# Normalising a tile in four interleaved steps instead of three, in the second layer of a fused attention and two-layer kernel

## The chip, the cores and the metric

One core of a Trainium2 chip runs the whole program: threshold attention, a first layer and a second layer. The metric is the device time of one execution in microseconds, the median of several. TensorE multiplies matrices into PSUM banks; VectorE, ScalarE and GpSimd do the element-wise work; SyncE issues the DMAs. Each engine takes its instructions strictly in the order in which the program gives them.

## The reference

The attention output becomes an array of 2304 rows of 512, then two layers follow. The change touches the second:

```
x = attention(q, k, v, tau)                    # -> (2304, 512)
g = where(h >= 1, h, where(h <= -1, 0, (h + 1)**2 / 4)),  h = x @ w_in1    # 2048 wide
x = g @ w_out1                                 # (2304, 512)

h   = x @ w_in2                                # (2304, 1024)
e   = exp(h - max(h));  sm = e / (sum(e) + 1e-9)          # per row
s   = h * sm
ln  = (s - mean(s)) / sqrt(var(s) + 1e-6) * g_ln
out = ln @ w_out2                              # (2304, 512)
```

## The kernel before

The first layer ends with an array x in SBUF, feature by token. The second layer takes the 2304 tokens as 18 tiles of 128, in 9 pairs. Each value is split in two halves, a high and a low one, and each product is three matmuls (high by high, high by low, low by high) over each part of the contraction.

**The first matrix product** of a pair k (tiles 2k and 2k+1) is done by seven half-sized products, `product(k, 1)` to `product(k, 7)` (L979), after the scheme that needs seven block products instead of eight. Each is six matmuls of 128x512. The left factors are sums of blocks of x: `y_adds` (L934) makes them on VectorE, four adds of 128x256, and `y_split` (L943) makes the high half on ScalarE (L948) and the low half on GpSimd (L949). `product(k, 1)` leaves its bank to a ScalarE copy (L994), and products 6, 7 and 4 add to the same bank afterwards; 5 is copied by L998 and 3 adds to its bank; 6 is copied by L1000. Products 2, 3 and 7 end in an add with a maximum on VectorE (L975), 4 in a maximum (L1006).

**The normalisation** of a tile i is a generator, `moe2_ln` (L1008), and `ln_step(i)` (L1210) issues it to the next yield. Step 1: the negative maximum on VectorE (L1015) and two exponentials with sums on ScalarE (L1018). Step 2: the sum and its reciprocal (L1022, L1023), two products h * e / sum with sums on VectorE (L1026), the mean (L1030) and a square with its sum on ScalarE (L1031). Step 3: the variance (L1033), its power -0.5 on GpSimd (L1034), a correction of three short instructions on VectorE (L1035 to L1037), the multiply over 128x1024 (L1038), and, for all but the two first and the two last tiles, `moe2_shuffle` (L1048): a VectorE transpose within blocks (L1052) and four DMA writes to DRAM (L1058).

**The second matrix product.** `moe2_fetch(i)` (L1066) loads a shuffled tile back in one DMA; `moe2_land(i)` (L1083) makes its high half on ScalarE (L1087) and its low half on GpSimd in two instructions (L1090). For the two first and the two last tiles `moe2_tr(i)` (L1095) does this with TensorE transposes instead, two ScalarE casts (L1108) and two VectorE subtractions (L1109). `moe2_out(i)` (L1126) is 24 matmuls (L1132), eight by eight: high by both halves of the weights, then low. `moe2_store(i)` (L1138) copies the bank on ScalarE (L1142) and issues the output DMAs on SyncE (L1144).

**The order.** The program is scheduled by hand: the order of the calls at the end of the kernel (L1281 to L1381) is each engine's order. Waits between engines come from the data dependencies. Pairs 0 to 2 are written out call by call; a loop over k = 3 to 8 follows (L1327), with o = 2k - 4, in which the products of pair k, the normalisation of tiles o+2 and o+3, the first step of tile 2k and the outputs o and o+1 stand side by side. "Output o" is `moe2_out(o)`, and (k,n) is `product(k, n)`. A part written out by hand follows the loop for the last tiles. `jobs.finish()` issues what is left of the preparation of the weights of the last product: in this execution one GpSimd subtraction (L552).

Of the kernel before, what the change touches and what calls it, by code (L numbers as in the profile page):

```python
# [21 lines left out]
def kernel(  # L22
# [82 lines left out]
    def f32(ap):  # L105
        return ap.bitcast(F32)
# [522 lines left out]
    def parts(*keys):  # L629
        return [lambda key=key, n=n: part(key, n) for key in keys for n in range(KD)]  # L630
# [66 lines left out]
    jobs = Jobs(parts(("in1", 0), ("out1", 0)), JOB_EVERY, 2)  # L697
# [29 lines left out]
    for b in range(B - 1):  # L727
        o = (b + 1) * NPAIR * UNITS
        at(late_, o + 6, recips_load, b, att_p)
        at(late_, o + 9, recips, b)  # L730
    for b in range(B - 1):
        for p in range(NPAIR):
            o = (b + 1) * NPAIR * UNITS + NORM[0] + NORM[1] * p
# [54 lines left out]
    X_AT, o = {}, 0  # L788
# [145 lines left out]
    def y_adds(k):  # L934
        r0, r1, pairs = y_views(k)
        a11, a12, a21, a22 = (x[:, h : h + KH, r] for r in (r0, r1) for h in (0, KH))
        s1, s2, s3, s4 = (t[:, h : h + KH, :] for t in pairs for h in (0, KH))
        nc.vector.tensor_tensor(s1, a21, a22, op=ALU.add)
        nc.vector.tensor_tensor(s3, a11, a21, op=ALU.subtract)
        nc.vector.tensor_tensor(s2, s1, a11, op=ALU.subtract)  # L940
        nc.vector.tensor_tensor(s4, a12, s2, op=ALU.subtract)

    def y_split(k, m):  # L943
        r0, r1, pairs = y_views(k)
        v = ([x[:, :, r0]] + pairs + [x[:, KH:KD, r1]])[m]
        n = v.shape[1]
        hi, lo = (t.rearrange("p (k t) -> p k t", k=n) for t in y_home(k, m))
        nc.scalar.copy(hi, v)  # L948
        nc.gpsimd.tensor_tensor(lo, v, f32(hi), op=ALU.subtract)  # L949
        for h in range(0, n, KH):  # L950
            y_t[k, 2 * m + h // KH] = hi[:, h : h + KH, :], lo[:, h : h + KH, :]
# [27 lines left out]
    def product(k, n):  # L979
        b, a, o = PRODUCTS[n]  # L980
        hi, lo = y_t[k, a]
        w = op_tile(o)
        ps = acc(k, b)
        first = n in (1, 2, 5)
        for kk in range(KH):
            for m, (st, at_) in enumerate(((hi, kk), (hi, KH + kk), (lo, kk))):
                nc.tensor.matmul(  # L987
                    ps, lhsT=st[:, kk, :], rhs=w[:, at_, :],
                    start=first and kk == 0 and m == 0, stop=kk == KH - 1 and m == 2,
                    skip_group_check=not first,  # L990
                )
        i = 2 * k
        if n == 1:
            nc.scalar.copy(so_half(i, 0), ps)  # L994
        elif n == 2:
            add_max(i, 0, ps)
        elif n == 5:
            nc.scalar.copy(so_half(i + 1, 1), ps)  # L998
        elif n == 6:
            nc.scalar.copy(so_half(i, 1), ps)  # L1000
        elif n == 7:
            add_max(i + 1, 1, ps)
        elif n == 3:
            add_max(i, 1, ps)
        else:
            nc.vector.tensor_reduce(maximum(i + 1, 0), ps, axis=AXES.X, op=ALU.max)  # L1006

    def moe2_ln(i):  # L1008
        st = g_p.tile([P, 10], F32, tag="st", name="st", bufs=3)
        e = keep["e"][:, i % 2, :]  # L1010
        so = keep["so"][i // 2 % 2][:, i % 2, :]
        half = [slice(HF * g, HF * g + HF) for g in range(2)]
        h = [so[:, half[0]] if i % 2 == 0 else acc_t[i // 2, 0], so[:, half[1]]]
        nmax, sm, mu, va, rs, t1 = (st[:, n : n + 1] for n in range(6))
        nc.vector.tensor_scalar(nmax, maximum(i, 0), maximum(i, 1), -1.0, op0=ALU.max, op1=ALU.mult)  # L1015
        two = [st[:, n : n + 1] for n in range(8, 10)]
        for g in range(2):
            nc.scalar.activation(  # L1018
                out=e[:, half[g]], in_=h[g], func=ACTF.Exp, bias=nmax, scale=1.0, accum_out=two[g]
            )  # L1020
        yield
        nc.vector.tensor_scalar(sm, two[0], two[1], 1e-9, op0=ALU.add, op1=ALU.add)  # L1022
        nc.vector.reciprocal(sm, sm)  # L1023
        two = [st[:, n : n + 1] for n in range(6, 8)]
        for g in range(2):
            nc.vector.scalar_tensor_tensor(  # L1026
                out=so[:, half[g]], in0=h[g], scalar=sm, in1=e[:, half[g]], op0=ALU.mult, op1=ALU.mult,
                accum_out=two[g],
            )
        nc.vector.tensor_scalar(mu, two[0], two[1], -1.0 / FF2, op0=ALU.add, op1=ALU.mult)  # L1030
        nc.scalar.activation(out=e, in_=so, func=ACTF.Square, bias=mu, scale=1.0, accum_out=va)  # L1031
        yield
        nc.vector.tensor_scalar(va, va, 1.0 / FF2, 1e-6, op0=ALU.mult, op1=ALU.add)  # L1033
        nc.gpsimd.tensor_tensor(rs, va, mhalf, op=ALU.pow)  # L1034
        nc.vector.tensor_scalar(t1, rs, rs, va, op0=ALU.mult, op1=ALU.mult)  # L1035
        nc.vector.tensor_scalar(t1, t1, -0.5, 1.5, op0=ALU.mult, op1=ALU.add)
        nc.vector.tensor_tensor(rs, rs, t1, op=ALU.mult)  # L1037
        nc.vector.tensor_scalar(so, so, mu, rs, op0=ALU.add, op1=ALU.mult)  # L1038
        ln_t[i] = e, so
        if i not in ON_PE:  # L1040
            moe2_shuffle(i)
        yield
# [23 lines left out]
    def moe2_fetch(i):  # L1066
        land = land_t[i] = raw_p.tile([P, FF2], F32, tag="raw", name="land")
        nc.sync.dma_start(land, sq_t.pop(i))
# [26 lines left out]
    def moe2_tr(i):  # L1095
        _, so = ln_t.pop(i)
        if i > 1:
            t = wga_p.tile([P, 2, FF2], F32R, tag="wg", name="ln")
            hi, lo = t[:, 0, :], [t[:, 1, 0:T], t[:, 1, T:FF2]]
        else:  # L1100
            hi, lo = split_tiles(i)
        for g in range(2):
            o = slice(T * g, T * g + T)
            ps = y_bank(3 + g if i == 0 else 1 + g, "lt")
            for f in range(KD):
                r = slice(f * P, f * P + P)
                nc.tensor.transpose(ps[:, r], so[:, T * g + f * P : T * g + f * P + P], ident)  # L1107
            nc.scalar.copy(hi[:, o], ps)  # L1108
            nc.vector.tensor_tensor(lo[g], ps, f32(hi[:, o]), op=ALU.subtract)  # L1109
        lt_t[i] = halves(hi, lo)  # L1110
# [27 lines left out]
    def moe2_store(i):  # L1138
        if i not in o_ps:
            return  # L1140
        o = wt_p.tile([P, DM], F32, tag="w", name="o")
        nc.scalar.copy(o, o_ps.pop(i))  # L1142
        for r, rows in out_rows(i):
            nc.sync.dma_start(rows, o[r, :])  # L1144
# [55 lines left out]
    jobs = Jobs([], 0, 3)  # L1200
# [9 lines left out]
    def ln_step(i):  # L1210
        if 0 <= i < NTT:
            if i not in ln:
                ln[i] = moe2_ln(i)
            next(ln[i])
# [68 lines left out]
    product(1, 1)  # L1283
    product(1, 5)
    ln_step(1)
    y_adds(2)
    product(1, 2)
    ln_step(0)
    product(1, 6)
    for m in range(2):  # L1290
        y_split(2, m)
# [1 line left out]
    product(1, 3)  # L1293
    product(1, 7)
    moe2_tr(0)
    ln_step(1)
    for m in range(2, 4):
        y_split(2, m)
    jobs.finish()
    ln_step(2)  # L1300
    product(2, 1)
    ln_step(2)
    ln_step(2)
    moe2_fetch(2)
    product(2, 2)
    product(1, 4)
    moe2_out(0)
    moe2_tr(1)
    product(2, 5)
    product(2, 6)  # L1310
    y_split(3, 0)
    ln_step(3)
    product(2, 3)
    y_adds(3)
    y_split(3, 1)
    ln_step(3)
    moe2_store(0)
    moe2_out(1)
    product(2, 7)
    ln_step(3)  # L1320
    moe2_fetch(3)
    for m in range(2, 4):
        y_split(3, m)
    moe2_land(2)
    ln_step(4)
    ln_step(4)
    for k in range(3, NPR):  # L1327
        o = 2 * k - 4
        last = k == NPR - 1
        if k > 3:  # L1330
            product(k - 1, 7)
        ln_step(o + 2)
        moe2_fetch(o + 2)
        product(k, 1)
        moe2_store(o - 1)
        product(k, 5)
        product(k, 2)
        product(k - 1, 4)
        moe2_land(o + 1)
        ln_step(o + 3)  # L1340
        if k == 3:
            moe2_out(o)
            product(k, 6)
        ln_step(o + 3)
        if not last:
            y_adds(k + 1)
        ln_step(o + 3)
        moe2_fetch(o + 3)
        if not last:
            for m in range(4):  # L1350
                y_split(k + 1, m)
        if k > 3:
            moe2_out(o)
            product(k, 6)
        product(k, 3)
        moe2_store(o)
        moe2_land(o + 2)
        ln_step(2 * k)
        if last:
            moe2_out(o + 1, slice(0, 12))  # L1360
            product(k, 7)
        ln_step(2 * k)
        moe2_out(o + 1, slice(12 * last, None))
    i = NTT - 2
    product(NPR - 1, 4)
    ln_step(i)
    ln_step(i + 1)
    moe2_land(i - 1)
    moe2_store(i - 3)
    moe2_out(i - 2)  # L1370
    ln_step(i + 1)
    moe2_tr(i)
    ln_step(i + 1)
# [40 lines left out]
```

## Time and profile before

| | |
|---|---|
| median of 3 runs | 974.01 us (971.22 to 975.45) |
| the profiled execution, its own time | 973.01 us |
| its span, first to last instruction | 971.2 us |
| mean granted TensorE clock | 0.996 of full speed |
| busy: TensorE / VectorE / ScalarE / GpSimd | 97% / 68% / 56% / 64% |

The second layer takes the last fifth of the span, from about 760 us on. In the rows further on, PE is TensorE's matmuls, PEld its weight loads, DVE is VectorE, ACT is ScalarE, POOL is GpSimd and SPq is the queue of SyncE, which issues DMAs. A row of a timeline gives the start and the duration in us, the engine, the line, the operation, output and inputs, the shape and the count; the bracket holds the idle time of the engine before it and what ended it.

### The profile page before, as it was taken

Reading aid. Unit: us, or ns where it says so; the run is one execution under the profiler, and the core shown is the slowest. Engines: PE = TensorE matmul, PEld = TensorE weight load, DVE = VectorE, ACT = ScalarE, POOL = GpSimd, SP = SyncE. Lnnn points to the kernel's source line nnn. Section 1 sums busy time; section 2 is a strip of 40 time slices with the busy share of each in tenths; the row PEclk is TensorE's granted clock in tenths of the full one; section 3 lists DMA queues with packets and bytes.
Section 4 is the critical chain, followed back from the end, with each engine's and each line's share of the span. In section 5 each row is a group of like instructions: output and inputs, shape, how many; then the busy total and the mean of one; then the engine's idle time right before and its main releaser. Section 6 shows DMA issues by size and latency. Waiting matters only on the chain. (4 is left out here: it accounts for less than half of the span.)

```text
span 971.2 us, 15226 instructions
## 1 busy us (share of the span) xinstructions
PE 939.4 (97%) x5261; PEld 836.4 (86%) x5261; DVE 661.8 (68%) x1109; ACT 543.7 (56%) x1019; POOL 623.8 (64%) x605
## 2 busy tenths in 40 slices
PE   7999999999999999999999999999999999799997
PEld 7899999998999988889888988898889977588885
DVE  5687887877878764567665775668456576777762
ACT  3677777777777684555443534444343455555542
POOL 6677888988798897776465545546466644455421
PEclk9999999999999999999999999999999999999999
DMA  5565667656665413212411141113121003534442
GB/s 139 141 152 117 153 151 172 152 146 152 152 153 124 112 44 99 89 44 74 155 65 61 49 149 65 57 66 119 54 77 33 22 13 108 137 112 120 123 139 54
DMA packets 89437, 100.65 MB, mean 104 GB/s; under 512 B 49968, under 2 KB 61552, under 8 KB 89360
## 3 DMA queue, kind: packets, MB, share of 16 engines
q1 hardware_dynamic: 87664, 99.02, 38.1%
q8 instruction: 41, 0.67, 0.3%
q10 hardware_dynamic: 1696, 0.66, 0.3%
q14 instruction: 36, 0.29, 0.1%
HBM read 55.65 MB, written 16.40 MB: 74 GB/s over the span
## 5 line engine op out<-in xcount | busy, mean ns | idle before, releaser
L429 POOL TENSOR_TENSOR plo<-e,phi 128x576 fp32r<-128x576 f32 x144 | 205.9, 1438 | 49.7 <-ACT phi L428 46.7
L873 POOL TENSOR_TENSOR gl<-cl,gh 128x512 fp32r<-128x512 f32 (+1 forms) x80 | 97.2, 1216 | 152.1 <-ACT gh L872 92.6
L890 PE MATMUL y<-gh,wg 128*128 128x512 f32 (+1 forms) x640 | 184.6, 369 | 0.0
L850 PE MATMUL h<-xs,wg 128*128 128x512 f32 (+1 forms) x768 | 164.4, 362 | 0.0
L420 DVE SCALAR_TENSOR_TENSOR e<-zt,ntau,e 128x576 f32<-128x576 f32 x144 | 117.2, 814 | 68.9 <-ACT e L415 48.5
L850 PEld LDWEIGHTS h<-xs,wg 128*128 128x128 f32 x768 | 139.6, 188 | 16.3
L890 PEld LDWEIGHTS y<-gh,wg 128*128 128x128 f32 x640 | 118.5, 188 | 16.0
L415 ACT ACTIVATE e<-zt 128x576 f32<-128x576 f32 x144 | 93.9, 652 | 67.8 <-PE zt L402 53.5
L338 DVE TENSOR_REDUCE mcol<-sc 128x1 f32<-128x576 f32 x160 | 116.7, 748 | 4.0 <-PE sc L325 3.8
L890 PE MATMUL y<-gl,wg 128*128 128x512 f32 (+1 forms) x320 | 118.4, 370 | 0.0
L1132 PE MATMUL o<-xs,ln 128*128 128x512 f32 x432 | 103.7, 395 | 1.6 <-ACT o L1142 1.2
L872 ACT CAST gh<-cl 128x512 fp32r<-128x512 f32 (+1 forms) x80 | 46.0, 576 | 105.1 <-DVE cl L871 98.2
L868 DVE TENSOR_SCALAR cl<-h 128x512 f32<-128x512 f32 (+1 forms) x80 | 50.7, 634 | 76.1 <-PE h L850 70.3
L1132 PEld LDWEIGHTS o<-xs,ln 128*128 128x128 f32 x432 | 81.6, 190 | 21.1 <-ACT o L1142 1.5
L428 ACT CAST phi<-e 128x576 fp32r<-128x576 f32 x144 | 96.3, 669 | 1.4 <-ACT mt L368 0.7
L869 ACT ACTIVATE cl<-cl,half 128x512 f32<-128x512 f32 (+1 forms) x80 | 54.3, 679 | 73.5 <-DVE cl L868 72.0
L325 PE MATMUL sc<-k_both,q_st 128*128 128x288 f32 x320 | 72.5, 308 | 7.6 <-DMA q_st<-lo 3.2
L402 PE MATMUL zt<-q_st,k_both 128*128 128x288 f32 x320 | 72.9, 309 | 3.2 <-DVE lo L279 2.8
L452 PE MATMUL av<-phi,v_hi 128*128 128x288 f32 x320 | 71.3, 304 | 1.8 <-ACT xs L464 1.8
L523 POOL TENSOR_TENSOR dec_a<-dec_a,raw 128x512 uint32<-128x512 uint32 x48 | 65.8, 1371 | 8.3 <-DVE dec_a L519 5.5
L452 PE MATMUL av<-plo,v_hi 128*128 128x288 f32 x320 | 69.4, 298 | 1.3 <-POOL plo L429 1.3
L452 PE MATMUL av<-phi,v_lo 128*64 128x288 f32 x320 | 69.4, 298 | 0.0
(149 smaller groups left out, 1894.0 us busy)
## 6 DMA issues: line engine op xcount, KB each, us to landing
raw<-in_moe_w_in_dram SPq DMA_DIRECT2D x24, 512.0 KB
raw<-in_moe_w_out_dram SPq DMA_DIRECT2D x24, 512.0 KB
k_both<-q_st SPq DMA_DIRECT2D x30, 288.0 KB
sq<-e SPq DMA_DIRECT2D x56, 128.0 KB
land<-sq SPq DMA_DIRECT2D x14, 512.0 KB
k_both<-lo SPq DMA_DIRECT2D x32, 144.0 KB
q_st<-lo SPq DMA_DIRECT2D x32, 144.0 KB
x<-xs SPq DMA_DIRECT2D x32, 144.0 KB
```

The source lines that it names most:

```text
L325: nc.tensor.matmul(ps[:, c, 0:HS], lhsT=st[j][i][r, n * P : n * P + P], rhs=kk[j][i][r, o + c * HS : o + (c + 1) * HS], start=(st is q_st) ...
L338: nc.vector.tensor_reduce(mc[:, n : n + 1], sc_ps.pop((h, n))[:, :, 0:HS], axis=AXES.XY, op=ALU.max, negate=True)
L402: nc.tensor.matmul(ps[:, c, 0:HS], lhsT=st, rhs=mv[:, c * HS : (c + 1) * HS], start=(m == 0), stop=(m == len(todo) - 1),)
L415: nc.scalar.activation(out=e, in_=st_ps[u][:, :, 0:HS], func=ACTF.Exp)
L420: nc.vector.scalar_tensor_tensor(out=e, in0=st_ps.pop(u)[:, :, 0:HS], scalar=ntau[:, 0:1], in1=e, op0=ALU.is_ge, op1=ALU.mult)
L428: nc.scalar.copy(hi, e)
L429: (nc.vector if u - NU in LO_DVE or u < NU - UNITS and u % UNITS in LO_UNITS else nc.gpsimd).tensor_tensor(lo, e, f32(hi), op=ALU.subtract)
L452: nc.tensor.matmul(ps[0:o, c, 0:HS], lhsT=vv, rhs=pp[:, c, :], start=first and pp is hi and o == P, stop=last and pp is lo,)
L850: nc.tensor.matmul(ps, lhsT=a[:, kk, f], rhs=m[:, kk, :], start=(n == 0 and kk == 0), stop=(n == 2 and kk == KD - 1),)
L873: nc.gpsimd.tensor_tensor(gl, cl, f32(gh), op=ALU.subtract)
L890: nc.tensor.matmul(y_ps[c][d], lhsT=a[:, jj, ds_], rhs=m, start=(jj == 0 and n == 0), stop=(jj == JG - 1 and n == 2),)
L1132: nc.tensor.matmul(o_ps[i], lhsT=a[f], rhs=wg_t["out2", f // 4][m][:, f % 4, :], start=(n == 0), stop=(n == len(terms) - 1))
```

## The change

The generator gets one more yield, so that a tile's normalisation has four steps, and the calls are put in another order. In the loop, the fourth step of tile o+2 comes after the first of tile o+3, the fourth of tile o+3 after the first of tile 2k, and `y_split(k+1, 0)` comes ahead of `y_adds(k+1)`; outputs and products keep their order among each other, but for output 1, which now follows (2,7).

```diff
@@ moe2_ln
         nc.gpsimd.tensor_tensor(rs, va, mhalf, op=ALU.pow)
+        yield
         nc.vector.tensor_scalar(t1, rs, rs, va, op0=ALU.mult, op1=ALU.mult)
@@ after the first layer
     ln_step(1)
-    y_adds(2)
+    jobs.finish()
+    ln_step(0)
     product(1, 2)
     ln_step(0)
+    y_adds(2)
     product(1, 6)
     for m in range(2):
         y_split(2, m)
@@
     product(1, 3)
     product(1, 7)
     moe2_tr(0)
+    ln_step(2)
+    ln_step(1)
     ln_step(1)
     for m in range(2, 4):
         y_split(2, m)
-    jobs.finish()
-    ln_step(2)
     product(2, 1)
     ln_step(2)
+    product(2, 2)
+    product(1, 4)
+    ln_step(2)
+    ln_step(3)
     ln_step(2)
     moe2_fetch(2)
-    product(2, 2)
-    product(1, 4)
     moe2_out(0)
     moe2_tr(1)
     product(2, 5)
     product(2, 6)
     y_split(3, 0)
     ln_step(3)
+    y_adds(3)
     product(2, 3)
-    y_adds(3)
     y_split(3, 1)
+    product(2, 7)
     ln_step(3)
+    ln_step(4)
     moe2_store(0)
     moe2_out(1)
-    product(2, 7)
     ln_step(3)
     moe2_fetch(3)
     for m in range(2, 4):
         y_split(3, m)
     moe2_land(2)
-    ln_step(4)
     ln_step(4)
@@ for k in range(3, NPR)
         if k > 3:
             product(k - 1, 7)
         ln_step(o + 2)
-        moe2_fetch(o + 2)
         product(k, 1)
         moe2_store(o - 1)
         product(k, 5)
         product(k, 2)
         product(k - 1, 4)
+        ln_step(o + 3)
         moe2_land(o + 1)
-        ln_step(o + 3)
-        if k == 3:
-            moe2_out(o)
-            product(k, 6)
+        ln_step(o + 2)
+        moe2_fetch(o + 2)
+        moe2_out(o)
+        if not last:
+            y_split(k + 1, 0)
         ln_step(o + 3)
         if not last:
             y_adds(k + 1)
+        product(k, 6)
+        ln_step(o + 3)
+        product(k, 3)
+        if not last:
+            for m in range(1, 4):
+                y_split(k + 1, m)
+        moe2_store(o)
+        ln_step(2 * k)
         ln_step(o + 3)
         moe2_fetch(o + 3)
-        if not last:
-            for m in range(4):
-                y_split(k + 1, m)
-        if k > 3:
-            moe2_out(o)
-            product(k, 6)
-        product(k, 3)
-        moe2_store(o)
         moe2_land(o + 2)
-        ln_step(2 * k)
         if last:
             moe2_out(o + 1, slice(0, 12))
             product(k, 7)
@@ after the loop, i = 16
     product(NPR - 1, 4)
     ln_step(i)
     ln_step(i + 1)
-    moe2_land(i - 1)
+    ln_step(i)
     moe2_store(i - 3)
     moe2_out(i - 2)
+    moe2_land(i - 1)
+    ln_step(i + 1)
     ln_step(i + 1)
     moe2_tr(i)
     ln_step(i + 1)
```

## Rows read from the trace of the kernel before

**Rows 1.** The page: busy us (share of the span) and instructions of each engine.

```profile
PE 939.4 (97%) x5261; PEld 836.4 (86%) x5261; DVE 661.8 (68%) x1109; ACT 543.7 (56%) x1019; POOL 623.8 (64%) x605
```

**Rows 2.** Stages: length; busy PE, PEld, DVE, ACT, POOL; granted clock, DMA share, GB/s.

```profile
860.00:880.00 20.00, 20.00 (x88) 16.28 (x87) 14.98 (x37) 10.60 (x22) 11.06 (x10) 1.00 0.43 117
...
838.00:842.00 4.00, 4.00 (x11) 3.14 (x12) 2.56 (x6) 3.09 (x6) 0.64 (x2) 0.57 0.50 185
```

**Rows 3.** Timeline of PE, second layer: the groups that this text speaks of.

```profile
778.28 4.44 PE L987 MATMUL h<-op,y 128*128 128x512 f32 x18 [0.38 <-ACT so L994]
...
794.22 4.41 PE L987 MATMUL h<-op,xs 128*128 128x512 f32 x18
...
817.82 3.05 PE L987 MATMUL h<-op,y 128*128 128x512 f32 x12 [1.18 <-ACT so L994]
...
829.68 3.94 PE L987 MATMUL h<-op,xs 128*128 128x512 f32 x16 [0.88 <-POOL xs L949]
837.92 2.38 PE L987 MATMUL h<-xs 128*128 128x512 f32 x6 [4.30 <-DVE mx L975]
...
948.41 11.33 PE L1132 MATMUL o<-xs,ln 128*128 128x512 f32 x48 [1.25 <-ACT o L1142]
```

**Rows 4.** The chain that ended last: start us, us, what (matmul pieces).

```profile
837.92 2.38 PE h L987 x6
840.31 6.32 PE o L1132 x24
...
939.44 1.39 PE h L987 x6
```

**Rows 5.** Waits, 755 to 972 us: us in total, times, longest us.

```profile
DVE st L1022 <- ACT e L1018: 23.1, 15, 1.6
...
DVE st L1035 <- POOL st L1034: 12.2, 18, 0.7
DVE st L1033 <- ACT e L1031: 9.5, 10, 1.4
```

**Rows 6.** Timeline of DVE: the end of tile 5's step 3, parts of tile 6's.

```profile
828.92 0.73 DVE L1037 TENSOR_TENSOR st<-st 128x1 f32<-128x1 f32 x1
829.68 1.75 DVE L1038 TENSOR_SCALAR so<-so,st 128x1024 f32<-128x1024 f32 x1
831.46 1.25 DVE L1052 STREAM_TRANSPOSE e<-so 128x1024 f32<-128x1024 f32 x1
...
835.13 0.21 DVE L1022 TENSOR_SCALAR st<-st 128x1 f32<-128x1 f32 x1 [1.59 <-ACT e L1018]
...
837.18 0.68 DVE L975 CUSTOM_DVE_ANT_0 so<-h,so 128x512 f32<-128x512 f32 x1
...
839.45 0.27 DVE L1035 TENSOR_SCALAR st<-st 128x1 f32<-128x1 f32 x1 [0.67 <-POOL st L1034]
...
839.95 0.16 DVE L1037 TENSOR_TENSOR st<-st 128x1 f32<-128x1 f32 x1
840.14 0.81 DVE L1038 TENSOR_SCALAR so<-so,st 128x1024 f32<-128x1024 f32 x1
```

**Rows 7.** Timeline of ACT: tile 0's square, copies of products, casts of landed tiles.

```profile
776.52 1.15 ACT L1031 ACTIVATE e<-so,st 128x1024 f32<-128x1024 f32 x1 [2.54 <-DVE st L1030]
...
796.07 0.60 ACT L998 COPY so<-h 128x512 f32<-128x512 f32 x1
...
817.20 0.56 ACT L994 COPY so<-h 128x512 f32<-128x512 f32 x1
...
840.78 1.05 ACT L1087 CAST ln<-land 128x1024 fp32r<-128x1024 f32 x1 [0.74 <-DMA land<-sq]
...
946.84 1.03 ACT L1087 CAST ln<-land 128x1024 fp32r<-128x1024 f32 x1
```

**Rows 8.** Groups of DVE, 847 to 930 us (busy us, mean ns | idle); one instruction of the tail.

```profile
L1026 DVE SCALAR_TENSOR_TENSOR so<-so,st,e 128x512 f32<-128x512 f32 x12 | 8.7, 749 | 0.1
...
948.09 1.68 DVE L1026 SCALAR_TENSOR_TENSOR so<-so,st,e 128x512 f32<-128x512 f32 x1
```

## The prediction

> **What bounds the kernel now.** I read the page's busy shares first: TensorE is busy 97% of the span, no other engine over 68% [rows 1]. So at most 3% can come from filling TensorE's gaps, and the question is which gaps lie where the diff edits. The table by stages shows a round of the second layer (one pair of tiles) in its steady state: TensorE 20.00 of 20 us, VectorE 14.98 [rows 2]. A round holds seven products of six matmuls and two output sums of 24, 90 matmuls; six take 1.39 us in the chain, 0.232 us each [rows 4], so 20.9 us. Nothing is to be had there.
>
> The gaps are in TensorE's timeline [rows 3]. In the order of time: 0.38 us ahead of product (1,6), 1.18 us ahead of (3,6), 0.88 us inside (4,1), 4.30 us ahead of (3,4), 1.25 us ahead of output 15. The reader is to see the releaser of each: a ScalarE copy, a GpSimd subtraction, a VectorE add-with-maximum, a ScalarE copy; never a transfer. And a second cost behind the 4.30: the granted clock, 1.00 elsewhere, is 0.57 from 838 to 842, mostly at 1.2 GHz [rows 2]. In the chain the six matmuls of (3,4) took 2.38 and the 24 of output 4 took 6.32 us [rows 4]: 8.70 against 30 x 0.232 = 6.96, so 1.74 us more.
>
> Why VectorE is late there: it runs in order, and before the change a tile's chain stands on it nearly without anything between. VectorE stood 23.1 us for the exponentials, 12.2 us for GpSimd's power (18 times, all tiles) and 9.5 us for the square [rows 5]: 44.8 us over nine pairs, 5 us a pair. With 15 us of work that makes a round of about 20 us, as long as TensorE's, so a lag, once there, is not made up. The add-with-maximum of (3,7), which frees the bank that (3,4) adds to, ran at 837.18 because step two of tile 6 stood ahead of it; that one started at 835.13, after 1.59 us of waiting for exponentials [rows 6], although (3,7) had long left TensorE.
>
> **The change, part by part.** No instruction is added or removed: 18 tiles keep the same work, DMAs included. One yield splits the old third step behind the power: step 3 is the scale of the variance and the power, step 4 the correction, the multiply, the transpose and four DMA writes. The rest is the order in each queue.
>
> *Hidden waits.* In the new round VectorE has the even tile's step 4 between the odd tile's steps 1 and 2, the sums of the next pair between its steps 2 and 3, and the odd tile's step 4 between the even tile's steps 1 and 2. Step 4 lasts from 839.45 over the 0.81 us multiply plus a 1.25 us transpose [rows 6], about 2.7 us, which covers the 1.6 us for exponentials; the power (0.67 us of waiting [rows 6]) lies behind a maximum or the sums. That gives VectorE 4 to 5 us a round. In the steady rounds TensorE is full, so it buys no time there; it buys slack.
>
> *The start, walked by hand.* Until the sums of pair 2 nothing differs. I count, by the rows of tile 6 [rows 6]: step 1 1.8 us, step 2 2.05 (835.13 to 837.18), the square with its hand-over 1.4, the power 0.8, step 4 1.5, or 2.5 with GpSimd beside it, the transpose 1.2, a maximum 0.65, the four sums some 1.5. Tile 0's square starts at 776.52 [rows 7]. GpSimd now has the last weight subtraction ahead of the power; with 1.3 to 1.75 us for it, tile 0 is normalised about 781, half a microsecond sooner than before; tile 1's step 2 comes behind the moved sums and ends near 784.5, 0.6 to 1.0 us later than now, and its maxima near 785.7. Product (1,4) needs them: from the row at 778.28 (three products, eight transposes, two products) it is due at 786.2, so the margin is some 0.5 us. From there tile 2's steps come early: step 2 ends near 792.5, its square 793.8, tile 3's exponentials 795.5 to 796.2, its transpose near 797.5.
>
> *A new wait.* Tile 3's exponentials now stand on ScalarE ahead of the two copies for tile 1's transposes and of the copy of (2,5). That copy ran at 796.07 [rows 7]; I get 796.4 to 797.2 for its start, so its end is 797.0 to 797.8. Product (2,3) adds to that bank and is the third of the 18 matmuls that start at 794.22 [rows 3], due at 797.0. Cost 0 to 1.2 us (the upper end with the 0.5 us margin of (1,4) overrun too); I take 0.35, the middle of my copy's times. Behind the copy stand (2,6)'s copy and a cast of pair 3; both have a product's time, 1.39 us, in hand. The swap of output 1 and (2,7) brings (2,7) 5.6 us forward and costs nothing.
>
> *Pairs 3 and 4.* Tile 3's transpose, which now ends near 812, comes to about 807.5; tile 4's square to 809 to 811, so the copy of (3,1), now at 817.20 [rows 7], comes by 812.7, while (3,6) is due at 816.5 to 817.2. The 1.18 us go. Pair 4's casts have the sums by 820 and are through GpSimd by 826; (4,1) needs only the first of them, which is moved ahead of the sums, and is due at 826.3 to 827: the 0.88 us go. The add-with-maximum of (3,7) ends by 828.7; (3,4) is due at 830.5 to 831.2. The 4.30 us go, and with the gap the 1.74 us of low clock behind it: minus 1.18 + 0.88 + 4.30 + 1.74 = 8.1. The nearest miss is 1.8 us at (3,4).
>
> *SyncE and DMA.* From the start of tile 5's transpose at 831.46 to the cast of the tile that came back by DMA, which waited for the landing and began at 840.78, it is 9.3 us [rows 6, 7]. In the new round the even tile's transpose starts 9 to 10 us after the round's start and its output is due at 28; the odd one's starts at 17 to 18 and is due at 36. Each has 8 us over. The store moved ahead of a fetch only shortens SyncE's wait. The next exponentials write the tile that the shuffle's DMAs read; those have left 4 to 5 us later, about when the exponentials are due. I cost it at nothing: the 3 us of slack in ScalarE's round cover it, and without that cover it is 1 us on ScalarE.
>
> *The tail.* Output 15 waited 1.25 us for a copy on ScalarE [rows 3], which stood behind tile 17's exponentials and a cast at 946.84 [rows 7]. Now the exponentials do not wait for tile 16's step 4 (1.5 us), and the copy precedes the cast. Next in line is that cast: had its data landed only at 946.84, it would end 0.7 us after TensorE is free. So 0.5 to 1.25 us; I take 1.0.
>
> **Sum.** 8.1 + 1.0 - 0.35 = 8.75 us. The profiled execution took 973.01 us (span 971.2 and 1.8 around it): 964.3. It lies 1.0 us under the median of the three runs, so for a median I say **965.0**. The runs before span 4.2 us, so about 0.5% is what a measurement can tell from no change.
>
> **A rule against it.** Tile 5's multiply took 1.75 us beside GpSimd's subtractions, tile 6's 0.81 us [rows 6]; more overlap can make more of the first kind. The Trainium skill, "SBUF — State Buffer", section "Who interferes with whom", says that VectorE and GpSimd share one port pair: a tensor_scalar in its two-port mode or an instruction with two SBUF inputs and a GpSimd operation exclude each other for their whole length. The trace agrees for the multiply. By that rule the even tiles' multiplies and the softmax products could be blocked as well; that case is rival (3).
>
> **The rivals.** (1) *The stall shrinks but stays.* ScalarE's new order costs the full 1.2 us at (2,3), and VectorE reaches (3,4) 2 us past its time. For it: the start rests on margins of 0.5 us. Against: the walk's late ends are in it already. Gain 8.75 - 0.85 - 2 - half the clock's 1.74 = 5.0: 969.
>
> (2) *The change does not hide what it says.* GpSimd's queue holds the power behind subtractions of 1.3 us, VectorE waits in step 4 instead, the 4.30 us and the clock stay. For it: three subtractions stand ahead of each odd power. Against: the sums and a maximum stand ahead of its use. Only 1.18 and 1.0 go: 972.
>
> (3) *Slower: VectorE becomes the bound.* In every steady round its instructions meet GpSimd's. Price: per tile 0.94 us at the multiply [rows 6], 0.57 at the correction's last step, 0.73 against 0.16 us [rows 6], and 2 x 0.93 at the softmax products, 1.68 against 0.75 us at the one place where it happened [rows 8]: 3.4 a tile, 6.7 a round. It decides from 20.9 us a round; 15.0 + 6.7 + 1 of waits left is 22.7, 1.8 too much, five rounds: +9, less the 2.2 that go anyway: 981. Against: twelve softmax products in the rounds of now average 749 ns [rows 8].
>
> **Chances.** Forecast 0.72, (1) 0.14, (2) 0.10, (3) 0.04. Faster by over 0.5% is below 969.1: nearly all of the forecast and somewhat over half of (1), 0.80; within 0.5%: the rest of (1) and (2), 0.16; slower 0.04. The range starts at 962.0 (all 9.35 us gone and the spread of the runs) and goes to 969.8, which takes in most of (1).
>
> **What would show it.** Right: TensorE full from 797.5 to the tail, the granted clock 1.00 there, (3,4) near 831, the copy of (3,1) near 811, no wait for ScalarE's copy at output 15, a gap under 1 us at (2,3). Wrong: a wait of over 1 us at (2,3), (1,4) or (3,4), a clock under 1.00 between 780 and 860, VectorE's multiply at 1.75 us in even tiles with a gap at every (k-1,4), or a cast of a landed tile that waits for its DMA with TensorE behind it.

## The result, and the profile after

The new kernel took 963.58 us (median of 6 runs, 961.72 to 966.44), the kernel before 973.03 us in the six runs beside it (970.87 to 975.45). The ratio is 0.9908, 95% interval 0.989 to 0.9925: faster by 0.9%, inside the range of 962.0 to 969.8 and 1.4 us under the forecast of 965.0.

The page's first part and the stages of the new kernel, with the columns of [rows 1] and [rows 2]:

```profile
PE 938.0 (98%) x5261; PEld 836.3 (87%) x5261; DVE 675.8 (70%) x1109; ACT 543.1 (56%) x1019; POOL 629.0 (65%) x605
```

```profile
860.00:880.00 20.00, 20.00 (x89) 16.34 (x88) 17.37 (x37) 11.40 (x23) 11.47 (x11) 1.00 0.47 125
...
838.00:842.00 4.00, 4.00 (x19) 3.23 (x18) 3.93 (x9) 1.77 (x4) 3.29 (x3) 1.00 0.57 132
```

TensorE is as full in a steady round as it was, and the granted clock is 1.00 where it had been 0.57. But VectorE, with the same instructions, is now busy 17.37 of 20 us instead of 14.98: each of some of them takes longer. That is followed up below.

TensorE's timeline of the new kernel, the groups with gaps and those that answer to [rows 3]:

```profile
766.52 2.94 PE L987 MATMUL h<-op,xs 128*128 128x512 f32 x12
...
777.49 4.43 PE L987 MATMUL h<-op,y 128*128 128x512 f32 x18 [0.38 <-ACT so L994]
...
783.53 2.99 PE L987 MATMUL h<-op,xs 128*128 128x512 f32 x12 [0.73 <-DVE so L1026]
...
797.67 3.06 PE L987 MATMUL h<-op,xs 128*128 128x512 f32 x12 [0.70 <-ACT so L998]
...
817.20 2.95 PE L987 MATMUL h<-op,y 128*128 128x512 f32 x12
...
826.97 4.29 PE L987 MATMUL h<-op,xs 128*128 128x512 f32 x18
831.52 1.66 PE L987 MATMUL h<-xs 128*128 128x512 f32 x6 [0.26 <-DVE mx L975]
...
838.48 2.95 PE L987 MATMUL h<-op,xs 128*128 128x512 f32 x12
...
938.87 11.31 PE L1133 MATMUL o<-xs,ln 128*128 128x512 f32 x48
...
951.29 5.76 PE L1133 MATMUL o<-xs,ln 128*128 128x512 f32 x24 [0.24 <-ACT ln L1109]
```

The reader is to see that the brackets at (3,6) (817.20), inside (4,1) (the row at 826.97) and at output 15 (938.87) are gone, that the 4.30 us at (3,4) are 0.26, and that two brackets are new: (2,1) waits 0.73 us for VectorE and (2,3) 0.70 us for ScalarE. The same two ends of the second layer in the kernel before, and between them the product behind output 4, (4,6), which is at 838.48 above:

```profile
767.31 2.94 PE L987 MATMUL h<-op,xs 128*128 128x512 f32 x12
...
846.47 2.95 PE L987 MATMUL h<-op,xs 128*128 128x512 f32 x12
...
960.85 5.76 PE L1132 MATMUL o<-xs,ln 128*128 128x512 f32 x24 [0.24 <-ACT ln L1108]
```

From product (0,3), the first of that group, to output 17 is 193.54 us before and 184.77 after, 8.77 less; the rest of the 9.5 us between the two spans lies ahead of the change (0.79 us at the start of (0,3)). I use this **stretch** for the experiments too, since it leaves out the long part of the kernel that no edit touches: the new kernel profiled again gave 184.78.

Where the 8.77 us arose, from the starts of the same groups in both traces:

| place | us gained |
|---|---|
| (2,1), new wait | -0.97 |
| output 0, no longer behind the last weight subtraction on GpSimd | +0.45 |
| (2,3), new wait | -1.01 |
| (3,6), gap gone | +1.36 |
| from there to (3,7) | +0.16 |
| (4,1) to (3,4), gaps gone but for 0.26 | +5.62 |
| (3,4) and output 4, clock at 1.00 | +1.59 |
| steady rounds, to (8,4) | +0.06 |
| output 15, gap gone | +1.49 |
| to output 17 | +0.02 |

A gap costs 0.2 to 0.3 us more than its bracket says, since the bracket counts from the modelled end of the last matmul.

The waits of the second layer in the new kernel, 755 to 962 us, with the columns of [rows 5]:

```profile
DVE st L1033 <- ACT e L1031: 8.9, 11, 1.4
...
DVE st L1036 <- POOL st L1034: 3.0, 4, 1.2
...
PE h L987 <- DVE so L1026: 0.7, 1, 0.7
```

The 23.1 us for exponentials have no row any more, the power's 12.2 us are 3.0, the square's 9.5 us are 8.9. So 33 of 45 us of VectorE's waits went, 3.7 us a pair.

### The profile page after: what moved, and what is told of

It reads as the page before. It is cut to its first block, busy times and chain, and to the rows that moved or that the text cites. A ratio compares the mean times of both kernels' runs of the same rounds, so it can differ in the third digit from the quotient of the medians.

```text
span 961.7 us, 15230 instructions
## 1 busy us (share of the span) xinstructions
PE 938.0 (98%) x5261; PEld 836.3 (87%) x5261; DVE 675.8 (70%) x1109; ACT 543.1 (56%) x1019; POOL 629.0 (65%) x605
## 5 line engine op out<-in xcount | busy, mean ns | idle before, releaser
L871 DVE TENSOR_TENSOR cl<-cl,h 128x512 f32<-128x512 f32 (+1 forms) x80 | 50.4, 630 | 27.5 <-ACT cl L869 27.5
```

## The experiments

**Which part carries it.** Each run has the new order in one part only; elsewhere the old order, with steps 3 and 4 called together. The edit is the diff shown above, cut to the part before the loop, the loop, or the part after it. The first:

> The new order stands only in the part written out before the loop; the loop and the tail are in the order of before (steps 3 and 4 called together). My theory (the lead comes from the part before the loop, where tile 3 is normalised 4.1 us earlier; the loop alone cannot make it): no gap at (3,6), the gaps of 0.73 us at (2,1) and 0.70 us at (2,3) as in the new kernel, and at (3,4) about 2.5 us left, since the add-with-maximum of (3,7), which ended at 837.86, comes 4.1 us earlier and the product is due near 831.3; some 4 us under the time of before, about 969. Rival (the interleaving in the loop does it all, by hiding waits): the gap at (3,4) stays 4 us or more and the time is within 1.5 us of before.

```profile
831.65 2.08 PE L987 MATMUL h<-xs 128*128 128x512 f32 x6 [1.93 <-DVE mx L975]
833.53 6.86 PE L1133 MATMUL o<-xs,ln 128*128 128x512 f32 x24
840.22 2.95 PE L987 MATMUL h<-op,xs 128*128 128x512 f32 x12
...
942.09 11.35 PE L1133 MATMUL o<-xs,ln 128*128 128x512 f32 x48 [1.21 <-ACT o L1143]
```

In these rows of its TensorE timeline the gap at (3,4) is 1.93 us, the tail's 1.21 is still there, and (3,6) has no bracket. Median 967.73 us against 972.61, ratio 0.995 (0.9933 to 0.9968); stretch 189.53, 4.0 less than before. The theory held, with the gap 0.6 us smaller than it said. The low clock is still there, at its full price: from (3,4) to (4,6), six matmuls and the 24 of output 4, it is 8.57 us here, 8.55 in the kernel before and 6.96 in the new one.

> The new order stands only in the loop over pairs 3 to 8. My theory: in the new kernel VectorE takes 20.3 us from the end of tile 4's step 2 (811.18) to the end of the add-with-maximum of (3,7) (831.46); from the later start of before (815.95) that gives 836.2, with (3,4) due at about 832.6, so the 1.18 us at (3,6) stay, the gap at (3,4) is still about 3.6 us with a low clock behind it, and the time is about 2 us under before, 971. Rival (the loop does it all): the gap at (3,4) is under 1 us, the clock stays at 1.00, and the time is 6 to 7 us under before, about 966.5.

```profile
818.95 3.05 PE L987 MATMUL h<-op,y 128*128 128x512 f32 x12 [1.18 <-ACT so L994]
823.03 5.86 PE L1133 MATMUL o<-xs,ln 128*128 128x512 f32 x24 [1.03 <-ACT ln L1088]
...
837.39 2.93 PE L987 MATMUL h<-xs 128*128 128x512 f32 x6 [2.98 <-DVE mx L975]
...
948.03 11.33 PE L1133 MATMUL o<-xs,ln 128*128 128x512 f32 x48 [0.23 <-ACT o L1143]
```

The loop's order alone leaves 2.98 us at (3,4), keeps the 1.18 at (3,6) and adds 1.03 at output 3, whose landed tile was fetched at 817.21 and cast at 821.95, straight behind tile 5's exponentials. The six matmuls behind the gap take 2.93 us, and the clock is low: 0.74 on the mean of 832 to 845 us; from (3,4) to (4,6) it is 9.78 us. Median 971.26, ratio 0.9975 (0.9961 to 0.9989); stretch 192.02, 1.5 less, of which 1.0 arose at output 15: its wait fell from 1.25 to 0.23 us, though the tail is in the old order. The rival falls: interleaving in the loop does not by itself remove the 4.30 us.

> The new order stands only in the part after the loop. My theory: the 1.25 us wait of output 15 for a ScalarE copy goes and nothing takes its place (the new kernel has no gap there), all other gaps as before: 1.3 to 1.5 us under before. Rival (the tail's gain in the new kernel came from VectorE's lead, not from the order of the tail): no change, the gap stays 1.0 us or more.

```profile
947.96 11.33 PE L1133 MATMUL o<-xs,ln 128*128 128x512 f32 x48 [0.50 <-ACT ln L1088]
```

Half and half: the copy no longer holds output 15, but the cast of landed tile 15 does, by 0.50 us. Stretch 192.76, 0.8 less; median 972.2, ratio 0.999 (0.9973 to 1.0008), no difference that the times can tell. In the new kernel this 0.50 is not there. With the loop's order alone 0.23 us of the wait was left, with the part ahead of the loop alone 1.21. So the tail's own order takes about half of the wait, the loop's order takes most of it, and the two together take all.

The three parts alone give 4.0 + 1.5 + 0.8 = 6.3 us of stretch, together 8.8: either of the first two alone still ends in a gap of 2 to 3 us at (3,4) with a low clock behind it, and the sum is missing that. From the run with the first part alone to the new kernel it is 4.8 us more: 1.6 for the rest of the gap at (3,4), 1.6 for the clock and 1.5 at output 15. So neither part carries the gain by itself: the part ahead of the loop gives the lead, and the loop keeps enough of it to reach (3,4).

**What the yield itself does.**

> The new order without the extra yield: the old steps 3 and 4 are called together where step 4 stands. My theory: the split itself hides only the wait for GpSimd's power, 0.67 us a tile, on an engine with some slack in the steady rounds; the order of the other steps carries the gain. The gap at (3,4) grows from 0.26 to about 1 to 1.5 us, time 0 to 2 us over the new kernel. Rival (four steps are what makes it): VectorE loses 1.4 us in every round, the gap at (3,4) is 3 us or more with a low clock, and the time is 4 us or more over the new kernel.

```diff
         nc.gpsimd.tensor_tensor(rs, va, mhalf, op=ALU.pow)
-        yield
         nc.vector.tensor_scalar(t1, rs, rs, va, op0=ALU.mult, op1=ALU.mult)
...
             product(k - 1, 7)
-        ln_step(o + 2)
...
         product(k, 6)
-        ln_step(o + 3)
```

The same was done to the third steps ahead of the loop and behind it. Median 1008.94 us, ratio 1.0392 (1.0365 to 1.0419), 45 us over the new kernel (stretch 228.85, 44.1 more). My theory was wrong, and the rival had the direction at about a tenth of the price. Its waits, with the columns of [rows 5]:

```profile
DVE st L1035 <- POOL st L1034: 56.0, 18, 5.7
```

GpSimd's timeline in one round:

```profile
846.75 2.54 POOL L1090 TENSOR_TENSOR ln<-land,ln 128x512 fp32r<-128x512 f32 x2 [11.04 <-ACT ln L1087]
849.24 0.55 POOL L1034 TENSOR_TENSOR st<-st,mhalf 128x1 f32<-128x1 f32 x1
```

VectorE's, just behind it:

```profile
849.83 0.27 DVE L1035 TENSOR_SCALAR st<-st 128x1 f32<-128x1 f32 x1 [5.66 <-POOL st L1034]
```

And TensorE's at the next (k-1,4), which is (4,4):

```profile
867.40 2.93 PE L987 MATMUL h<-xs 128*128 128x512 f32 x6 [3.81 <-DVE mx L975]
```

Where step 4 stands, the call puts the power behind the subtractions of a landed tile in GpSimd's queue; those wait for ScalarE's cast, which waits for exponentials. VectorE then stands 5.7 us for a power of 0.55 us, and (k-1,4) waits 4 to 6 us in each of five rounds, with a low clock behind it each time (2.92 or 2.93 us for its six matmuls). So a separate step 3 is worth far more here than the 0.67 us that it hides on VectorE: it keeps the power's early place in GpSimd's queue. (The old order had that place too, by calling all of step 3 early.) The mechanism is that of the prediction's rival (2), at a price that I had not seen. The new order with both steps called where step 3 stands was not run, so what the split is worth against that is open.

**How much slack VectorE has.** In both orders the transpose of each odd tile is done twice, 1.17 us more on VectorE in every round:

```diff
-        nc.vector.transpose(
+        for _ in range(1 + i % 2):
+            nc.vector.transpose(
```

> The kernel before with the VectorE transpose of every odd tile done twice (1.17 us more on VectorE in each round, same data). My theory (VectorE's round in the old order is as long as TensorE's, so it has no slack): the gap at (3,4) grows from 4.3 to 6 us or more, and every later (k-1,4) gets a gap of about 1.2 us; 6 to 8 us over the time of before. Rival (VectorE, busy 15 of 20 us, has 5 us to spare in the steady rounds in either order): no gap at the later (k-1,4), 2 to 3 us over before.

> The new kernel with the same doubled transpose in odd tiles. My theory (the new order leaves VectorE about 2 us a round in which it waits for TensorE: 0.76, 0.72 and 0.59 us in the steady rounds of the trace): tiles 3 and 5 bring the gap at (3,4) from 0.26 to about 2.6 us, and from pair 5 on there is no gap at (k-1,4); 2.5 to 4 us over the new kernel. Rival (the slack bought is eaten by GpSimd's share of the port, VectorE being busy 17.4 of 20 us now): gaps of about 1 us at each later (k-1,4), 6 us or more over the new kernel.

TensorE's gaps in the old order, at (3,6), (3,4), later (k-1,4) and output 15, and then in the new one, at (3,4):

```profile
821.20 4.62 PE L987 MATMUL h<-op,y 128*128 128x512 f32 x12 [2.48 <-ACT so L994]
...
842.63 2.93 PE L987 MATMUL h<-xs 128*128 128x512 f32 x6 [5.60 <-DVE mx L975]
...
887.51 1.65 PE L987 MATMUL h<-xs 128*128 128x512 f32 x6 [0.29 <-DVE mx L975]
...
909.98 1.65 PE L987 MATMUL h<-xs 128*128 128x512 f32 x6 [1.42 <-DVE mx L975]
...
932.42 1.66 PE L987 MATMUL h<-xs 128*128 128x512 f32 x6 [1.47 <-DVE mx L975]
...
959.52 11.33 PE L1133 MATMUL o<-xs,ln 128*128 128x512 f32 x48 [1.94 <-ACT o L1143]
```

```profile
834.08 1.65 PE L987 MATMUL h<-xs 128*128 128x512 f32 x6 [1.76 <-DVE mx L975]
```

Old order: median 983.15 us against 972.27, ratio 1.0112 (1.009 to 1.0133), more than expected, because (3,6) and output 15 wait longer too (2.48 and 1.94 us) and the clock is now low behind (3,6) as well, whose 12 matmuls took 4.62 us instead of 2.95; stretch 202.54, 9.0 more than without the doubling. The first later round still absorbed it, then the gaps grow to 1.4 us or a little more. New order: 968.03, ratio 0.995 (0.9922 to 0.9979); stretch 187.15, 2.4 more than the new kernel: 1.5 at (3,4), whose gap is 1.76 us and not the 2.6 of the theory, 0.6 at output 15 (a bracket of 0.37 us), and 0.25 in the last rounds, where no bracket stands. So VectorE's round had less than 1.2 us to spare and now has about that. (Of the three waits that the theory adds up, the 0.76 us is for the square on ScalarE and not for TensorE.) This is what the interleaving in the loop bought.

**Why VectorE's instructions got longer.** VectorE's timeline in a steady round of the new kernel: two of the four sums of the next pair, and the even tile's second softmax product:

```profile
859.58 1.26 DVE L938 TENSOR_TENSOR x<-x 128x256 f32<-128x256 f32 x1
860.77 1.51 DVE L939 TENSOR_TENSOR x<-x 128x256 f32<-128x256 f32 x1
862.20 0.41 DVE L940 TENSOR_TENSOR x<-x 128x256 f32<-128x256 f32 x1
...
869.16 1.77 DVE L1026 SCALAR_TENSOR_TENSOR so<-so,st,e 128x512 f32<-128x512 f32 x1
```

A sum takes 0.41 us or three times that; the softmax product averaged 0.749 us in the old rounds [rows 8].

> The new kernel with GpSimd's two subtractions of each landed tile replaced by two fills with zero, which read nothing: the low half of the normalised tiles 2 to 15 is left out of the last product. My theory (VectorE's busy time rose from 15.0 to 17.4 of 20 us because its two-input instructions now meet GpSimd's subtractions): in the steady rounds VectorE falls below 16.2 of 20 us, and the second softmax product of the even tile takes 0.75 us again, not 1.77. Rival (the instructions are slow from something else, such as ScalarE's or a DMA's access to the same tiles): VectorE stays at 17 or more. TensorE is full there, so neither expects more than 0.5 us of time.

```diff
-            nc.gpsimd.tensor_tensor(
-                lo[g]..., land[:, :, r], f32(hv[:, :, r]), op=ALU.subtract
-            )
+            nc.gpsimd.memset(f32(lo[g]), 0.0)
```

Its stage row, and the second softmax products of an odd tile and of the even one:

```profile
860.00:880.00 20.00, 20.00 (x89) 16.32 (x88) 14.55 (x39) 11.04 (x22) 7.96 (x10) 1.00 0.48 132
```

```profile
862.40 1.25 DVE L1026 SCALAR_TENSOR_TENSOR so<-so,st,e 128x512 f32<-128x512 f32 x1
...
871.71 0.75 DVE L1026 SCALAR_TENSOR_TENSOR so<-so,st,e 128x512 f32<-128x512 f32 x1
```

VectorE falls to 14.55 us, the even tile's product to 0.75, and the four sums are 0.42 each again; the fills run for 0.98 us a tile just ahead. One instruction got longer: the odd tile's second product, 0.75 us in the new kernel, takes 1.25, and GpSimd's subtraction of `y_split(k+1, 0)` now runs beside it (861.80 to 863.10). Its one run took 967.19 us, of which the part ahead of the second layer took some 4 us more than in the profile of the new kernel; the stretch is 184.17, 0.6 less, with no gap at (3,4), so that the 0.26 us left there go with the longer instructions. So the longer instructions come from GpSimd's subtractions, those of a landed tile or of a split, and not from ScalarE or DMA, which were left as they were. Per round the sums and the softmax product take 1.26 + 1.51 + 1.77 against 0.42 + 0.42 + 0.75 us, 2.95 us more: most of the 3.7 us a pair that the interleaving hid. That agrees with the Trainium skill, "SBUF — State Buffer", section "Who interferes with whom", for VectorE instructions with two SBUF inputs and a GpSimd instruction that reads SBUF; it also says that one that only writes does not collide. The trace agrees as far as it goes: hardly any such VectorE instruction ran beside these fills, but the correction's last step at 938.48 did, and took 0.16 us, against 0.64 to 0.70 beside subtractions in the new kernel.

**Against the gaps that are left.**

> The new kernel with three changes of order ahead of the loop, against the three gaps left there: (1,1) ahead of tile 0's step 2, the sums of pair 2 behind tile 1's step 2, tile 3's step 1 behind (2,5). My theory (behind these gaps the next limit is VectorE's lead at (3,4)): the gaps of 0.38, 0.73 and 0.70 us go, the one at (3,4) grows from 0.26 to about 1 us, 0.7 to 1.2 us under the new kernel. Rival (VectorE's lead grows with them): 1.8 us under it, no gap at (3,4).

```diff
-    ln_step(0)
-    product(0, 4)
     product(1, 1)
+    ln_step(0)
+    product(0, 4)
...
-    y_adds(2)
     product(1, 6)
-    for m in range(2):
-        y_split(2, m)
+    y_split(2, 0)
     ln_step(1)
+    y_adds(2)
+    y_split(2, 1)
...
     ln_step(2)
-    ln_step(3)
     ln_step(2)
...
     product(2, 5)
+    ln_step(3)
     product(2, 6)
```

```profile
800.79 2.27 PE L987 MATMUL h<-op,xs 128*128 128x512 f32 x6 [2.89 <-ACT so L1000]
```

A miss of both theories: the three gaps went, and a new one of 2.89 us came at (2,7), since the copy of (2,6) now stood behind the exponentials that I had moved. The clock fell behind it too: the 30 matmuls from there took 8.65 us. Median 966.33, ratio 0.9939 (0.9918 to 0.9959); stretch 186.67, 1.9 more than the new kernel.

> As start_fixed, and tile 3's step 3 ahead of the split of pair 3's second part, and in the loop the even tile's step 2 behind the maximum of (k-1,7), so that (k-1,4) does not wait for it. My theory: no gap over 0.1 us from (1,6) to the last transposes, 2 us under the new kernel, about 961.5. Rival (step 2 and step 3 of the even tile, now next to each other, make VectorE wait for the square and come late at (k,3)'s bank or at the outputs): a gap of over 0.5 us in every round.

```diff
-    y_split(3, 1)
-    product(2, 7)
     ln_step(3)
+    y_split(3, 1)
+    product(2, 7)
...
             product(k - 1, 7)
+            ln_step(o + 2)
         ln_step(o + 2)
...
         if last:
             moe2_out(o + 1, slice(0, 12))
             product(k, 7)
-        ln_step(2 * k)
+            ln_step(2 * k)
```

It kept the same mistake, 2.84 us at (2,7), and had no other gap up to the last transposes: median 965.35, ratio 0.9937 (0.9915 to 0.9959), stretch 186.40. Its stated 961.5 was not reached; the rival's gaps in every round did not come either.

> The new kernel unchanged, beside the next one on the same chip. All theories: 963 to 965 us, the gaps as before: 0.38, 0.73, 0.70 and 0.26 us.

> As all_fixed, but tile 3's step 1 stands behind (2,6), so that both copies, of (2,5) and (2,6), come ahead of its exponentials on ScalarE, and the sums and splits of pair 3 stand ahead of tile 3's step 2, in the time in which VectorE waits for the exponentials. My theory (in all_fixed the copy of (2,6) behind the exponentials took 2.84 us of TensorE's time, and nothing else stood against it): no gap over 0.1 us from (1,6) to the last transposes, 2 us under the new kernel, about 961.5. Rival (VectorE cannot follow a TensorE that is 2 us earlier): a gap of 1 us or more at a product of pair 3 or at output 2 or 3, time as the new kernel.

```diff
     product(2, 5)
-    ln_step(3)
     product(2, 6)
+    ln_step(3)
     y_split(3, 0)
-    ln_step(3)
     y_adds(3)
+    y_split(3, 1)
+    ln_step(3)
     product(2, 3)
     ln_step(3)
-    y_split(3, 1)
     product(2, 7)
```

TensorE's timeline, from tile 1's transposes to the end:

```profile
794.52 5.78 PE L987 MATMUL h<-op,xs 128*128 128x512 f32 x24
...
950.31 5.76 PE L1133 MATMUL o<-xs,ln 128*128 128x512 f32 x24 [0.24 <-ACT ln L1109]
```

The second of these rows has the only bracket in its whole second layer. The stretch is 181.76 us, 3.0 under the new kernel's 184.78 beside it, whose gaps were 0.38, 0.73, 0.72 and 0.30 us this time. VectorE does follow a TensorE that is earlier, so the rival falls. The medians are 962.91 us (959.34 to 965.87) and 963.64 us (962.05 to 972.39), the ratios to before 0.9894 (0.987 to 0.9919) and 0.992 (0.9893 to 0.9947): the intervals overlap, so that it beats the new kernel is shown by the trace and not by the times.

## Why the prediction was right

**The account.** TensorE's gaps and the low clock behind the 4.30 us were the whole of it, as predicted: no gain arose in the steady rounds (+0.06). That the total of 8.75 us met 8.77 so closely is luck: its errors come to about 1.8 us upward and 1.8 downward. (The last step of the sum is off as well: 964.3 and 1.0 make 965.3, not 965.0.)

**Terms that held.** (3,6) 1.18 predicted, 1.36 measured; (4,1) and (3,4) 5.18 and 5.62; the clock 1.74 and 1.59. The times of the walk held less well. They are on the axis of the kernel before, and the new trace reaches (0,3) 0.79 us earlier, so 0.79 is to be added to its times. The walk had the copy of (3,1) by 812.7, and it ran at 812.43, which is 813.2 on that axis; it had the maximum of (3,7) ready by 828.7, and it ended at 831.46, which is 832.25, some 3.5 us late. TensorE was late too, by 1.2 us more than the prediction allowed, so that the margin of 1.8 us became a gap of only 0.26. The step that was off there: I had let VectorE's four sums take 1.5 us and each of the two softmax products 0.75; with GpSimd beside them the sums took 3.5 us and the two products 2.5.

**Terms that were mis-sized.** Three rows of the start, in VectorE's timeline of the new kernel: the fourth sum of pair 2, and the two softmax products of tile 2:

```profile
780.86 1.41 DVE L941 TENSOR_TENSOR x<-x 128x256 f32<-128x256 f32 x1
...
790.15 1.39 DVE L1026 SCALAR_TENSOR_TENSOR so<-so,st,e 128x512 f32<-128x512 f32 x1
...
791.47 1.22 DVE L1026 SCALAR_TENSOR_TENSOR so<-so,st,e 128x512 f32<-128x512 f32 x1
```

(2,3): predicted 0.35 within 0 to 1.2, measured 1.01. The copy started at 797.01, on the walk's axis 797.8, which is 0.6 us behind the last time of the walk, 797.2. Tile 2's step 2 was late by then: its two products took 1.39 and 1.22 us instead of 0.75, with GpSimd's subtractions beside them (789.70 to 792.14). Output 15: 1.0 predicted, 1.49 measured; the landed tile was in time. The reason given was only half of it: the prediction credited the tail's order, and the loop's order takes most of that wait without it.

**What was missed.** (2,1) cost 0.97 us, and the prediction had it at nothing. It walked tile 1's step 2 to 784.5, 0.6 to 1.0 us late, and looked only at (1,4) for who needs it. The bank of pair 0 that step 2 reads is also the one that (2,1) writes, and (2,1) comes before (1,4). What made the read late enough to matter is again GpSimd: the fourth sum, just ahead of step 2, took 1.41 us and the other three 0.42, with subtractions beside it from 780.38 on. Without that 1.0 us the bank would have been read by 782.4, and TensorE was ready for it at 782.6 (an estimate from these rows; no run shows it by itself). Against the wait stood a gain that was missed as well: the last weight subtraction, moved ahead, had held output 0 by 0.45 us.

**The step on hidden waits** was right in kind, and its size is now known: 3.7 us a pair instead of "4 to 5", of which the longer VectorE instructions take back 2.95. That was the mechanism of rival (3), priced at 6.7 us a round; it came to less than half of that, at the sums rather than at the correction, and VectorE stayed under TensorE's 20.9 us. (The slow softmax product of [rows 8] was not the only one in the old order, as the prediction says: tile 3's, at 804.47, took 1.13 us.) The prediction said that the interleaving buys slack and no time in the steady rounds; the doubled transpose shows that slack. It did not say how the gain divides: the part ahead of the loop is worth 4.0 us alone, the loop 1.5 alone, most of that at output 15, and (3,4) is free only with both.

## What to carry to other kernels

When a step of one engine's chain is moved, follow each buffer and bank that it reads to its next writer, not only its result to the next reader: the wait that the prediction missed altogether was a write to a bank still being read. A short instruction on a helper engine is worth the place that its queue gives it; keep it ahead of anything that waits for a transfer, and let only what uses its result move. Before counting a hidden wait as gained, look which instructions of the two engines will now run at the same time.

## What the runs showed of the hardware

TensorE's granted clock fell after gaps shorter than the 4.30 us of the kernel before, and its price did not grow evenly with the gap. The six matmuls of (3,4) and the 24 of output 4 take 6.96 us at 1.00, in the new kernel. Behind 4.30 us of idle time, in the kernel before, they took 8.55; behind 1.93, with the new order ahead of the loop only, 8.57; behind 2.98, with the loop's order only, 9.78. So a gap of about 2 us already cost 1.6 us more than itself. The granted clock was 0.50 from 833.5 to 836 in the second of these runs, which is 1.2 GHz.

The length of the gap alone does not decide it. Behind 1.76 us, in the new kernel with doubled transposes, the clock stayed at 1.00; so it did behind the 1.94 us at output 15 in the old order with doubled transposes, while it fell behind the 1.93 us above.
